# Second MoE of a talking-heads and double-MoE kernel: two token passes, seven block products in the second, weights narrowed once

## The chip, the cores and the metric

The kernel runs on one core of a Trainium2 chip. The metric is the device time of one execution in microseconds (us), lower being better. Engine names are those of the profile: PE is TensorE's matmuls, PEld its weight loads, DVE is VectorE, ACT ScalarE, POOL GpSimd and SP SyncE, which here only issues DMAs.

## The reference, cut to what matters

Three stages follow one another: an attention in which the heads are mixed before and after the softmax, a MoE with a SoLU and a layer norm (1792 tokens, 768 to 1024 to 768), and a second MoE with a squared ReLU (768 to 2048 to 768). The change is about the third, and prepares for it in the second.

```python
def _moe_ref(x, w_in, w_out, g_ln):
    h = x @ w_in
    e = np.exp(h - np.max(h, axis=-1, keepdims=True))
    solu = h * (e / (np.sum(e, axis=-1, keepdims=True) + 1e-09))
    mu = np.mean(solu, axis=-1, keepdims=True)
    var = np.mean((solu - mu) ** 2, axis=-1, keepdims=True)
    return ((solu - mu) / np.sqrt(var + 1e-06) * g_ln) @ w_out

def _moe2_ref(x, w_in, w_out):
    r = np.maximum(x @ w_in, 0.0)
    return (r * r) @ w_out
```

All weights of both MoEs come in as 64-bit floats; the kernel narrows them to 32 bits by moving bits about. Every product is made to 32-bit accuracy from two parts of each operand, a rounded one ("hi") and what is left ("lo"): hi*hi, hi*lo and lo*hi, so three matmuls where one would do.

## The kernel before, in words

Every engine does its instructions in the order in which the code issues them; nothing reorders them. `filler()` calls scattered through the code let pieces of background work (generators in `fill`) advance by one step.

**Attention** (up to about 405 us) reads q, k and v, and beside that narrows the first MoE's weights to DRAM, 48 pieces of 128x256 (`narrow_w1`). Each has an ACT square (L76), three DVE bit operations (L79, L83, L87) and two POOL operations (L96, L97).

**First MoE** (to 649 us) goes over 14 tiles of 128 tokens. For tile m, `h1` multiplies the tokens with w_in: 36 matmuls of 512 columns. `norm1` then takes the maximum (DVE L704), the exponential (ACT L707), the SoLU product (DVE L710), mean and variance (DVE L713, L715; POOL L717, L718), and normalises in place (DVE L720). `zt(m-1)` transposes the tile before on PE and splits it. From tile 4 on two `out1` calls follow, 24 matmuls of up to 384 columns each; a group of three tiles is one `out1` width. PE's order in a tile is thus h1(m), zt(m-1), out1, out1.

**Second MoE** (649 to 1120 us) walks over 8 slices e of 256 hidden units, and in each over five token groups (256 tokens, then four of 384; `GRP`). `h2(e, q)` makes the first product of a slice and a group, 18 matmuls for each of the two halves of the slice; ACT and DVE square it and split it into `g`; `y2(e, q)` makes the second product, 12 matmuls of 384 columns for each 128 tokens, and DVE adds it to a running sum `y` in SBUF (L955). The weights of slice e+1 are narrowed by `piece_w2` during slice e, 8 pieces of 128x384, with their hi and lo parts in the pool wi2 (left end of SBUF) for even slices and m2 (right end) for odd ones. The tokens, loaded once and split by `load_x2`, stay in SBUF: groups 0 and 1 in wi2, 2 to 4 in m2.

```python
    steps = [(e, q) for e in range(NE) for q in range(len(GRP))]
    h2(*steps[0])
    for i, (e, q) in enumerate(steps):
        ...
        if i + 1 < len(steps):
            h2(*steps[i + 1])
        y2(e, q)
```

PE thus always has the next group's first product between a group's squares and its second product.

Of the kernel before, what the change touches and what calls it, by code (L numbers as in the profile page):

```python
# [18 lines left out]
def kernel(  # L19
# [36 lines left out]
    const = ctx.enter_context(tc.tile_pool(name="const", bufs=1, side="left"))  # L56
    dram = ctx.enter_context(tc.tile_pool(name="dram", bufs=1, space=bass.MemoryType.DRAM))
# [601 lines left out]
    late.__exit__(None, None, None)  # L659

# [3 lines left out]
    m1_p = m1.__enter__()  # L664
    psi = tc.tile_pool(name="psi", bufs=1, side="left", space=PSUM, reuse_waits="tile")
# [34 lines left out]
    def norm1(m):  # L700
        ps = hps.pop(m)
        hv = ps.rearrange("p u f -> p (u f)")
        nm = m1_p.tile([128, 1], F32, tag="nm", name="nm", bufs=2)
        nc.vector.tensor_reduce(out=nm, in_=hv, op=ALU.max, axis=AX.X, negate=True)  # L704
        e = m1_p.tile([128, F1], F32, tag="e", name="e", bufs=2)
        sm = m1_p.tile([128, 1], F32, tag="sm", name="sm", bufs=2)
# [37 lines left out]
    def out1(grp, cc):  # L744
# [13 lines left out]
        o = m1_p.tile([128, GT * 128], F32, tag="o", name="o1", bufs=2)  # L758
        nc.scalar.copy(o[:, 0:width], ps[:, 0:width])
        nc.sync.dma_start(out=x2D[cc * 128:(cc + 1) * 128, t0:t0 + width], in_=o[:, 0:width])  # L760

    NTILE = NT // 128
    xr = {}
    wr = {}
    outs = []
    for m in range(NTILE):
# [5 lines left out]
        next(norm)  # L772
        if m > 0:
            zt(m - 1)
        run(norm)
# [17 lines left out]
    FE = 256
    NE = F2 // FE
    KE = FE // 128
    TG = 384
    GRP = [(0, NT % TG)] + [(t0, TG) for t0 in range(NT % TG, NT, TG)]
    x2 = {}
    w2 = {}

    def load_x2(g, pool):

        t0, n = GRP[g]
        t = pool.tile([128, 2, CC, n], F32R, name=f"x2_{g}")
        x2[g] = t
        rs = []
        for i in range(CC + 2):
            if i < CC:
                r = wi2_p.tile([128, TG], F32, tag="x2r", name="x2r", bufs=3)
                nc.sync.dma_start(out=r[:, 0:n], in_=x2D[i * 128:(i + 1) * 128, t0:t0 + n])  # L810
                rs.append(r)
            if i >= 2:
                c = i - 2
# [227 lines left out]
```

## Time and profile before

| what | value |
|---|---|
| median of 3 runs | 1122.43 us (1118.15 to 1130.88) |
| profiled execution, its own time | 1125.69 us |
| its span, first to last instruction | 1123.9 us |
| PE busy | 95% of the span |
| DVE, ACT, POOL busy | 61%, 42%, 37% |
| granted TensorE clock, mean | 0.983 |

The span is 1.8 us less than the execution's own time. Engine shares are means over three stages with different limits, so they are to be read by stage; matmuls are pipelined, and the pace of a run of them is read from the start of one run to the start of the next, divided by the count.

### The profile page before, as it was taken

Reading aid. Unit: us, or ns where it says so; the run is one execution under the profiler, and the core shown is the slowest. Engines: PE = TensorE matmul, PEld = TensorE weight load, DVE = VectorE, ACT = ScalarE, POOL = GpSimd, SP = SyncE. Lnnn points to the kernel's source line nnn. Section 1 sums busy time; section 2 is a strip of 40 time slices with the busy share of each in tenths; the row PEclk is TensorE's granted clock in tenths of the full one; section 3 lists DMA queues with packets and bytes.
Section 4 is the critical chain, followed back from the end, with each engine's and each line's share of the span. In section 5 each row is a group of like instructions: output and inputs, shape, how many; then the busy total and the mean of one; then the engine's idle time right before and its main releaser. Section 6 shows DMA issues by size and latency. Waiting matters only on the chain.

```text
span 1123.9 us, 30801 instructions
## 1 busy us (share of the span) xinstructions
PE 1067.6 (95%) x12920; PEld 926.9 (82%) x12920; DVE 680.8 (61%) x1201; ACT 468.9 (42%) x1026; POOL 418.7 (37%) x645
## 2 busy tenths in 40 slices
PE   8889889888898899999999999999999999999998
PEld 3566556655566688998989999999999999999998
DVE  2557676766676637443533786476676666766734
ACT  4556566666686634221211465322222223223210
POOL 2557797877584837111100653011111111111100
PEclk8989899999999999999999999999999999999999
DMA  6767688788676633111111653021111121111113
GB/s 179 206 187 236 210 232 246 240 233 237 182 226 180 189 103 116 57 31 55 36 36 48 193 183 113 29 57 43 57 57 57 50 63 43 57 57 57 29 71 127
DMA packets 95643, 135.00 MB, mean 120 GB/s; under 512 B 20720, under 2 KB 80368, under 8 KB 95504
## 3 DMA queue, kind: packets, MB, share of 16 engines
q1 hardware_dynamic: 86660, 108.50, 31.9%
q0 software_dynamic: 6464, 22.60, 7.1%
q10 hardware_dynamic: 2380, 1.93, 0.6%
q8 instruction: 102, 1.67, 0.6%
q14 instruction: 37, 0.30, 0.1%
HBM read 71.65 MB, written 22.81 MB: 84 GB/s over the span
## 4 chain that ended last, share of the span: by engine, by line
PE 85%; DMA 4%; issue 4%; ACT 3%; POOL 2%; DVE 1%; SPq 0%; ACTq 0%; POOLq 0%; DVEq 0%
PE ps_y L944 20%; PE ps_h L905 20%; PE ps_o L751 10%; PE ps_h L453 10%; PE ps_ring L293 6%; PE ps_ring L332 6%; PE ps_ring L202 5%; PE ps_pre L236 5%; DMA sdst<-ssrc 4%; ACT ssrc L209 1%; PE ps_tr L737 1%; ACT e L254 1%; POOL w1i L441 0%; PE ps_spare L481 0%; POOL sm L265 0%
## 5 line engine op out<-in xcount | busy, mean ns | idle before, releaser
L905 PE MATMUL ps_h<-x,ti 128*128 128x384 f32 (+1 forms) x1440 | 241.5, 325 | 0.0
L944 PE MATMUL ps_y<-to,g 128*128 128x384 f32 x1332 | 240.3, 337 | 0.2 <-ACT y L953 0.2
L905 PEld LDWEIGHTS ps_h<-x,ti 128*128 128x128 f32 x1440 | 236.5, 188 | 0.0
L944 PEld LDWEIGHTS ps_y<-to,g 128*128 128x128 f32 x1332 | 232.1, 188 | 2.2 <-DVE y L955 1.7
L293 PEld LDWEIGHTS ps_ring<-w,e 60*64 60x64 f32 (+1 forms) x5760 | 104.1, 139 | 70.3 <-issue 38.6
L312 DVE COPY at<-ps_ring 128x420 f32<-128x420 f32 x156 | 87.8, 610 | 102.6 <-PE ps_ring L293 102.5
L293 PE MATMUL ps_ring<-w,e 60*64 60x60 f32 (+2 forms) x5760 | 112.5, 223 | 30.0 <-issue 17.0
L209 ACT COPY ssrc<-ps_ring 128x896 f32<-128x896 f32 x92 | 82.5, 910 | 110.4 <-PE ps_ring L202 90.0
L913 ACT ACTIVATE r<-ps_h 128x384 f32<-128x384 f32 (+1 forms) x80 | 37.5, 469 | 215.2 <-PE ps_h L905 215.1
L453 PE MATMUL ps_h<-w1i,xs 128*128 128x512 f32 x504 | 120.5, 396 | 0.0
L751 PE MATMUL ps_o<-zt,w1o 128*128 128x384 f32 (+1 forms) x720 | 119.9, 325 | 0.0
L254 ACT ACTIVATE e<-ps_pre,nm 128x448 f32<-128x448 f32 x180 | 113.4, 641 | 13.8 <-DVE nm L247 12.1
L914 DVE SCALAR_TENSOR_TENSOR r<-ps_h,r 128x384 f32<-128x384 f32 (+1 forms) x80 | 42.4, 530 | 122.8 <-ACT r L913 122.7
L751 PEld LDWEIGHTS ps_o<-zt,w1o 128*128 128x128 f32 x720 | 116.8, 189 | 0.0
L453 PEld LDWEIGHTS ps_h<-w1i,xs 128*128 128x128 f32 x504 | 94.2, 188 | 21.5
L247 DVE TENSOR_REDUCE nm<-ps_pre 128x1 f32<-128x448 f32 x180 | 102.8, 611 | 15.1 <-PE ps_pre L236 15.0
L955 DVE TENSOR_TENSOR y<-ps_y,y 128x768 f32<-128x768 f32 x97 | 92.4, 953 | 31.8 <-PE ps_y L944 31.8
L861 POOL TENSOR_TENSOR ti<-wt,ti 128x384 fp32r<-128x384 f32 x32 | 34.4, 1075 | 206.6 <-ACT ti L860 206.6
L202 PE MATMUL ps_ring<-k,q 64*64 64x448 f32 x752 | 100.1, 569 | 8.0 <-issue 4.2
L332 PEld LDWEIGHTS ps_ring<-at,v 128*64 128x64 f32 x1536 | 77.7, 141 | 29.9 <-PE ps_pre L236 10.6
L236 PE MATMUL ps_pre<-sdst,wpre_bd 64*64 64x448 f32 x720 | 97.4, 580 | 5.1 <-issue 2.9
L332 PE MATMUL ps_ring<-at,v 128*64 128x120 f32 (+1 forms) x1536 | 85.2, 268 | 7.2 <-issue 4.3
(90 smaller groups left out, 1190.4 us busy)
## 6 DMA issues: line engine op xcount, KB each, us to landing
sdst<-ssrc SPq DMA_DIRECT2D x166, 210.0 KB
wr<-in_moe_w_in_dram SPq DMA_DIRECT2D x32, 384.0 KB
wr<-in_moe_w_out_dram SPq DMA_DIRECT2D x32, 384.0 KB
w1raw<-in_moe_w_in_dram POOLq DMA_DIRECT2D x24, 256.0 KB, 5.2
w1raw<-in_moe_w_out_dram POOLq DMA_DIRECT2D x24, 256.0 KB, 5.7
out_dram<-y SPq DMA_DIRECT2D x13, 384.0 KB
v<-in_v_dram POOLq DMA_DIRECT2D x12, 384.0 KB, 6.1
xraw<-xD SPq DMA_DIRECT2D x12, 384.0 KB
```

What stands on the lines that cost most here:

```text
L202: nc.tensor.matmul(out=ps[64 * u:64 * u + 64, e, 0:S], lhsT=qq[c][64 * e:64 * e + 64, p * n + u * half:p * n + u * half + 64], rhs=k[64 * ...
L209: (nc.vector.tensor_copy if dve else nc.scalar.copy)(ssrc[c][:, p:H:HP, :], ps[:, :, 0:S])
L236: nc.tensor.matmul(out=ps[b][64 * u:64 * u + 64, 0:S], lhsT=wpre_bd[64 * r:64 * r + m], rhs=ds[b][64 * r:64 * r + m], start=True, stop=True,)
L247: nc.vector.tensor_reduce(out=nm, in_=pres[s][b][:, 0:S], op=ALU.max, axis=AX.X, negate=True)
L254: nc.scalar.activation(out=e, in_=pres[s][b][:, 0:S], func=AF.Exp, bias=nms.pop((s, b)), scale=1.0, accum_out=sms[s][:, b:b + 1])
L293: nc.tensor.matmul(out=ps[64 * c:64 * c + 64, u, i0:i0 + ng * RH], lhsT=e[64 * u:64 * u + m, o:o + 64], rhs=w[64 * u:64 * u + m, b, g0:g0 ...
L332: nc.tensor.matmul(out=ps[64 * e:64 * e + 64, 0, q * 120:q * 120 + n], lhsT=t[:, g] if j < NJ else t[:, e, p], rhs=at[c][:, j * H + (g if ...
L453: nc.tensor.matmul(out=ps[:, u], lhsT=t[:, a, cc], rhs=w1i[cc][:, w, u * 512:(u + 1) * 512], start=(cc == 0 and a == 0 and w == 0), stop=( ...
L751: nc.tensor.matmul(out=ps[:, 0:width], lhsT=w1o[k][:, w, cc * 128:(cc + 1) * 128], rhs=zT[:, a, k, 0:width], start=(k == 0 and i == 0), st ...
L905: nc.tensor.matmul(out=ps[:, 0:n], lhsT=ti[:, w, cc, f * 128:(f + 1) * 128], rhs=x2[q][:, a, cc], start=(cc == 0 and i == 0), stop=(cc == ...
L944: nc.tensor.matmul(out=ps[:, u - us[0], 0:DM // 2], lhsT=g[:, a, f, o:o + 128], rhs=to[:, w, f, u * (DM // 2):(u + 1) * (DM // 2)], start= ...
L955: nc.vector.tensor_tensor(out=yo, in0=po, in1=yo, op=ALU.add)
```

## The change

The second MoE now makes two passes over 896 tokens each, and in each pass goes over all 8 slices (q = 0 to 15, `SEQ_P` and `SEQ`). A slice's first product is seen as a 2x2 block product: two halves of the hidden units (f), two halves of the tokens (t, 448 each), two halves of the 768 inputs (k). In the first pass (q < 8) each of the four result blocks is the sum of two block products ("22", "21", "12", "11"; 18 matmuls of 448 columns each). In the second pass the four blocks come from seven block products p1 to p7 of sums of blocks (9 matmuls each): POOL makes the sums of weights (`mix_w`), DVE the sums of tokens, once, to DRAM (`mix_second`), and DVE and ACT combine the products (`after`). p3, p2 and p4 are accumulated in PSUM on banks that already hold p5, p1 and p7.

The weights are no longer narrowed in the second MoE by `piece_w2`; `w2stream` narrows them once, to DRAM (w2iD, w2oD), 96 pieces of 128x256: 60 in the first MoE from its fifth tile on, six pieces (18 steps) a tile, and 36 in the first six slices of the first pass. A piece has an ACT square, one POOL operation and three DVE bit operations. Both passes read the narrowed weights back (`load_ra`, `load_ro`) and split them. The hi and lo parts for the second product (`to`) and the squares (`gt`) both lie in m2; the weights for the first product lie in wi2a at the left end, and the tokens in wi2 beside them, but for the blocks of p1, p5 and p6 in the second pass, which lie in m2. In the first MoE the normalisation moves from DVE to ACT, after a small DVE operation (`nb`). Tiles that were in `const` or m1 move to other pools.

```diff
-        nc.vector.tensor_scalar(
-            out=e, in0=e, scalar1=mv[:, 0:1], scalar2=rs, op0=ALU.subtract, op1=ALU.mult
+        nb = m1b_p.tile([128, 1], F32, tag="nb", name="nb", bufs=2)
+        nc.vector.scalar_tensor_tensor(
+            out=nb, in0=mv[:, 0:1], scalar=-1.0, in1=rs, op0=ALU.mult, op1=ALU.mult
         )
+        yield True
+        nc.scalar.activation(out=e, in_=e, func=AF.Identity, bias=nb, scale=rs)
...
+        def mask(i):
+            if i in todo:
+                t = ts[i] = home(i, False)
+                nc.scalar.activation(out=t, in_=words(i)[1].bitcast(F32), func=AF.Square)
+                nc.gpsimd.tensor_scalar(
+                    out=t, in0=t, scalar1=2.0**-30, scalar2=2.0 - 2.0**-23, op0=ALU.is_ge, op1=ALU.mult
+                )
...
+        for i in todo:
+            load(i + nr - 1)
+            mask(i + 2)
+            low, high = words(i)
+            bits = ts[i].bitcast(U32)
+            stt = nc.vector.scalar_tensor_tensor
+            stt(out=bits, in0=high, scalar=3, in1=bits, op0=ALU.logical_shift_left, op1=ALU.bitwise_and)
+            yield True
+            if ready:
+                store()
+            stt(out=bits, in0=high, scalar=0xC0000000, in1=bits, op0=ALU.bitwise_and, op1=ALU.bitwise_or)
+            yield True
+            stt(out=bits, in0=low, scalar=29, in1=bits, op0=ALU.logical_shift_right, op1=ALU.bitwise_or)
+            raws.pop(i)
+            ready.append(i)
+            yield True
...
+        steps2(rate(m, 4))
+        next(norm)
         if m > 0:
             zt(m - 1)
-        run(norm)
+        if m <= GT:
+            run(norm)
+        steps2(rate(m, 6))
...
+        pairs = PLAIN.get(name, ((name, name),))
+        for j, (tn, xn) in enumerate(pairs):
+            t = ti[q, tn]
+            for c in range(HC):
                 for i, (w, a) in enumerate(((0, 0), (0, 1), (1, 0))):
                     nc.tensor.matmul(
...
+                        out=bank[b][:, 0:HT],
+                        lhsT=t[:, w, c],
+                        rhs=xc[xn][:, a, c],
...
+    YO = [4, 5, 6, 3, 0, 1, 2]
+    SEQ = ["p1", "p6", 4, "p5", 5, "p7", 6, 3, 0, "p3", 1, 2, "p2", "p4"]
+    SEQ_P = ["22", 4, "21", 5, 6, 3, "12", 0, 1, 2, "11"]
...
+            at(3, split_ti, n, "p1")
+            at(3, mix_w, n, 0)
+            at(4, mix_w, n, 1)
+            at(5, split_ti, n, "p6")
+            at(6, split_ti, n, "p5")
+            at(7, lambda q: square(hs.pop(q), 1, 1), q)
+            at(7, split_ti, n, "p7")
+            at(8, split_to, q, 0)
+            at(10, split_ti, n, "p3")
+            at(11, split_to, q, 1)
+            at(11, load_ro, n)
+            at(12, split_ti, n, "p2")
+            at(13, split_ti, n, "p4")
+            at(13, load_ra, n + 1)
```

In `SEQ` and `SEQ_P` a number is a tile of 128 tokens whose second product (`y2`), that of the slice before, stands there; the work of `plan` is issued behind the place with its number.

On PE a slice of the second MoE stood so before (ps_h is the first product, ps_y the second, x the tokens, ti and to the weights of the first and second product):

```order
L905 MATMUL ps_h_12253<-x_0_9173,ti 128x256 x18
L905 MATMUL ps_h_12286<-x_0_9173,ti 128x256 x18
L944 MATMUL ps_y<-to,g 128x384 x36
L905 MATMUL ps_h_12360<-x_1_9354,ti 128x384 x18
L905 MATMUL ps_h_12391<-x_1_9354,ti 128x384 x18
L944 MATMUL ps_y<-to,g 128x384 x24
L905 MATMUL ps_h_12455<-x_2_9615,ti 128x384 x18
L905 MATMUL ps_h_12481<-x_2_9615,ti 128x384 x18
L944 MATMUL ps_y<-to,g 128x384 x36
```

A slice of the second pass now stands so, from p1 to p4 (xc is a block, or a sum of blocks, of the tokens):

```order
L1107 MATMUL ps_h_13407<-xc,ti 128x448 x9
L1107 MATMUL ps_h_13419<-xc,ti 128x448 x9
L1178 MATMUL ps_y<-to,gt 128x384 x12
L1107 MATMUL ps_h_13444<-xc,ti 128x448 x9
L1178 MATMUL ps_y<-to,gt 128x384 x12
L1107 MATMUL ps_h_13481<-xc,ti 128x448 x9
L1178 MATMUL ps_y<-to,gt 128x384 x36
L1107 MATMUL ps_h_13444<-xc,ti 128x448 x9
L1178 MATMUL ps_y<-to,gt 128x384 x24
L1107 MATMUL ps_h_13407<-xc,ti 128x448 x9
L1107 MATMUL ps_h_13481<-xc,ti 128x448 x9
```

Per slice and pass there are 63 matmuls of 448 columns here, 72 in the first pass, and over both passes 1080 for the 1440 of before; those of the second product are 1344 as before. The banks ps_h_13444, 13407 and 13481 come up twice, for the accumulated products.

On DVE a tile of the first MoE stood so before (nm to st is the normalisation up to mean and variance, zt the split of the tile before):

```order
L704 TENSOR_REDUCE nm<-ps_h 128x1
L708 TENSOR_SCALAR sm<-sm 128x1
L709 RECIPROCAL sm<-sm 128x1
L710 SCALAR_TENSOR_TENSOR e<-e,sm,ps_h 128x1024
L713 BN_STATS st<-e 128x6 x2
L715 BN_AGGR mv<-st 128x2
L740 TENSOR_TENSOR zt<-ps_tr,zt 128x4x128 x2
L720 TENSOR_SCALAR e<-e,mv,rs 128x1024
```

Now, from the statistics of a tile (from the fifth on) to the first steps behind the split (nraw is a raw piece of weights, nt its narrowed form):

```order
L725 BN_AGGR mv<-st 128x2
L828 SCALAR_TENSOR_TENSOR nt<-nraw,nt 128x256
L832 SCALAR_TENSOR_TENSOR nt<-nraw,nt 128x256
L834 SCALAR_TENSOR_TENSOR nt<-nraw,nt 128x256
L828 SCALAR_TENSOR_TENSOR nt<-nraw,nt 128x256
L731 SCALAR_TENSOR_TENSOR nb<-mv,rs 128x1
L753 TENSOR_TENSOR zt<-ps_tr,zt 128x4x128 x2
L832 SCALAR_TENSOR_TENSOR nt<-nraw,nt 128x256
L834 SCALAR_TENSOR_TENSOR nt<-nraw,nt 128x256
```

The normalisation has left DVE, and 18 narrowing steps a tile have come in, four of them ahead of `nb` and the split.

On SP's queue in the first pass, a slice's worth of DMAs now stands so; the second MoE's queue of before held the raw weights in the same way, but no reads of narrowed ones:

```order
L996 DMA ro<-w2oD 128x768 x2
L793 DMA nraw<-in_moe_w_in_dram 128x256
L985 DMA ra<-w2iD 128x3x256 x2
L811 DMA w2iD<-nt 128x256
L793 DMA nraw<-in_moe_w_in_dram 128x256
L811 DMA w2iD<-nt 128x256
L793 DMA nraw<-in_moe_w_out_dram 128x256
```

The reads ro and ra take up single buffers, and raw loads and stores of the stream stand behind them.

## Rows read from the trace of the kernel before

**Rows 1.** Stretches of the two MoEs: length, busy time by engine, PEclk, DMA share, GB/s.

```profile
core 0: us, PE busy (x) PEld busy (x) DVE busy (x) ACT busy (x) POOL busy (x), PEclk, DMA share, GB/s
446.90:604.70 157.80, 157.80 (x824) 142.57 (x822) 66.13 (x90) 34.04 (x62) 23.57 (x28) 1.00 0.14 43
...
648.70:1120.30 471.60, 471.42 (x2786) 469.12 (x2784) 300.52 (x493) 146.91 (x309) 72.92 (x69) 1.00 0.21 66
```

**Rows 2.** Second MoE, PE in order of time: start us, us, line, tiles, count.

```profile
701.97 4.39 PE L905 MATMUL ps_h<-x,ti 128*128 128x256 f32 x36
706.19 6.41 PE L944 MATMUL ps_y<-to,g 128*128 128x384 f32 x36
712.43 6.40 PE L905 MATMUL ps_h<-x,ti 128*128 128x384 f32 x36
...
781.55 6.52 PE L905 MATMUL ps_h<-x,ti 128*128 128x384 f32 x36
787.91 2.28 PE L944 MATMUL ps_y<-to,g 128*128 128x384 f32 x12
```

**Rows 3.** Matmuls by shape: count | busy us, mean ns | idle before.

```profile
L944 PE MATMUL ps_y<-to,g 128*128 128x384 f32 x1332 | 240.3, 337 | 0.2 <-ACT y L953 0.2
L905 PE MATMUL ps_h<-x,ti 128*128 128x384 f32 x1152 | 206.3, 336 | 0.0
...
L905 PE MATMUL ps_h<-x,ti 128*128 128x256 f32 x288 | 35.4, 281 | 0.0
```

**Rows 4.** First MoE, PE in order of time, one tile.

```profile
561.02 8.58 PE L453 MATMUL ps_h<-w1i,xs 128*128 128x512 f32 x36
569.44 1.03 PE L737 MATMUL ps_tr<-id_sb,e 128*128 128x128 f32 x8
570.23 8.57 PE L751 MATMUL ps_o<-zt,w1o 128*128 128x384 f32 x48
578.64 8.58 PE L453 MATMUL ps_h<-w1i,xs 128*128 128x512 f32 x36
```

**Rows 5.** First MoE, groups of instructions from 480 to 600 us.

```profile
L720 DVE TENSOR_SCALAR e<-e,mv,rs 128x1024 f32<-128x1024 f32 x7 | 13.9, 1983 | 0.0
...
L707 ACT ACTIVATE e<-ps_h,nm 128x1024 f32<-128x1024 f32 x7 | 7.8, 1117 | 64.1 <-DVE nm L704 64.1
```

**Rows 6.** Start of the first MoE, PE's transposes of tile 0 and their wait.

```profile
418.10 1.06 PE L737 MATMUL ps_tr<-id_sb,e 128*128 128x128 f32 x8 [1.15 <-DVE e L720]
```

**Rows 7.** Narrowing of 128x256 pieces in the attention: groups of instructions.

```profile
L96 POOL TENSOR_SCALAR w1sq<-w1sq 128x256 f32<-128x256 f32 x48 | 41.0, 854 | 4.0
...
L83 DVE SCALAR_TENSOR_TENSOR w1t<-w1raw,w1t 128x256 uint32<-128x256 uint32 x48 | 21.4, 445 | 1.4
...
L76 ACT ACTIVATE w1sq<-w1raw 128x256 f32<-128x256 f32 x48 | 19.8, 448 | 0.0
```

**Rows 8.** The same DVE operation: duration ns min/median/max, first and last start.

```profile
L83 DVE SCALAR_TENSOR_TENSOR w1t<-w1raw,w1t x48: 408/426/940, 65.9 to 324.6; 128x256 uint32<-128x256 uint32 x48
```

**Rows 9.** A stretch of the attention.

```profile
100.00:200.00 100.00, 89.44 (x2271) 59.62 (x2267) 72.30 (x162) 63.04 (x150) 79.55 (x144) 0.95 0.78 230
```

**Rows 10.** Second MoE, groups of instructions on DVE, POOL and ACT.

```profile
L955 DVE TENSOR_TENSOR y<-ps_y,y 128x768 f32<-128x768 f32 x97 | 92.4, 953 | 31.8 <-PE ps_y L944 31.8
...
L914 DVE SCALAR_TENSOR_TENSOR r<-ps_h,r 128x384 f32<-128x384 f32 x64 | 35.6, 557 | 104.3 <-ACT r L913 104.3
...
L861 POOL TENSOR_TENSOR ti<-wt,ti 128x384 fp32r<-128x384 f32 x32 | 34.4, 1075 | 206.6 <-ACT ti L860 206.6
...
L919 ACT CAST g<-r 128x384 fp32r<-128x384 f32 x64 | 32.8, 512 | 29.1 <-DVE r L914 29.1
```

**Rows 11.** SP's own waits: in total us, times, longest us.

```profile
SPq L832 <- DVE wt L87: 187.7, 25, 21.6
```

**Rows 12.** The last instructions: PE, the last sum on DVE.

```profile
1118.06 2.25 PE L944 MATMUL ps_ye<-to,g 128*128 128x384 f32 x12
...
1120.35 0.56 DVE L955 TENSOR_TENSOR y<-ps_ye,y 128x384 f32<-128x384 f32 x1 [0.49 <-PE ps_ye L944]
```

More of the change, by code (lines that the diff above doesn't have):

```diff
@@ L664 @@
     m1_p = m1.__enter__()
+    m1b = tc.tile_pool(name="m1b", bufs=1, side="right", reuse_waits="tile")
+    m1b_p = m1b.__enter__()
     psi = tc.tile_pool(name="psi", bufs=1, side="left", space=PSUM, reuse_waits="tile")
@@ L763, with home1, rate, steps2 @@
+    def home1(i, raw):
+        if raw:
+            return m1b_p.tile([128, WP], I64, tag="nraw", name="nraw", bufs=5)
+        return m1b_p.tile([128, WP], F32, tag="nt", name="nt", bufs=5)
+    stream = w2stream(range(FIRST), 5, home1)
+    NTILE = NT // 128
+    def rate(m, n):
+        return 0 if m <= GT else n if m < NTILE - 1 else n // 2
+    def steps2(n):
+        for _ in range(n):
+            next(stream, None)
     xr = {}
@@ L783 @@
             outs += [((m - 1) // GT - 1, cc) for cc in range(CC)]
-        for _ in range(2):
+        for i in range(2):
             if outs:
                 out1(*outs.pop(0))
+            if i == 0:
+                run(norm)
+            steps2(rate(m, 4))
+    outs += [((NTILE - 1) // GT, cc) for cc in range(CC)]
     wi1b.__exit__(None, None, None)
     wi1.__exit__(None, None, None)
+    wi2a = tc.tile_pool(name="wi2a", bufs=1, side="left", reuse_waits="tile")
+    wi2a_p = wi2a.__enter__()
@@ L791 @@
+    prep2 = prepare()
+    next(prep2)
+    steps2(4)
+    out1(*outs.pop(0))
+    zt(NTILE - 1)
+    run(stream)
+    m1b.__exit__(None, None, None)
     wi2 = tc.tile_pool(name="wi2", bufs=1, side="left", reuse_waits="tile")
     wi2_p = wi2.__enter__()
[L793 to L813, printed above, removed]
-                nc.scalar.copy(t[:, 0, c], rs[c][:, 0:n])
-                eng = nc.vector if g > 1 and c % 2 else nc.gpsimd
-                eng.tensor_tensor(
-                    out=t[:, 1, c], in0=rs[c][:, 0:n], in1=t[:, 0, c].bitcast(F32), op=ALU.subtract
-                )
-            yield True
@@ L863 @@
[L863 to L870 removed]
     for i, (g, cc) in enumerate(outs):
+        if i:
+            next(prep2, None)
         out1(g, cc)
[L873 to L878 removed]
@@ L879 @@
-    while fill:
-        filler()
-    for _ in x2q:
-        pass
-    for _ in x2q1:
-        pass
+    run(prep2)
     ps1.__exit__(None, None, None)
@@ L904, in h2, with prod @@
+    bank = {}
+    us = {}
+    hs = {}
+    low = []
+    def prod(q, name):
+        b = BANK[name]
+        first = name not in ("p3", "p2", "p4")
+        if first:
+            bank[b] = ps2_p.tile([128, 512], F32, tag=f"b{b}", name="ps_h2", bufs=1)
+        pairs = PLAIN.get(name, ((name, name),))
+        for j, (tn, xn) in enumerate(pairs):
+            t = ti[q, tn]
+            for c in range(HC):
                 for i, (w, a) in enumerate(((0, 0), (0, 1), (1, 0))):
                     nc.tensor.matmul(
-                        out=ps[:, 0:n],
@@ new lines, in prod, with lows @@
+                        lhsT=t[:, w, c],
+                        rhs=xc[xn][:, a, c],
+                        start=(first and j == 0 and c == 0 and i == 0),
+                        stop=(j == len(pairs) - 1 and c == HC - 1 and i == 2),
+                        skip_group_check=not first,
+                    )
+    def lows():
+        while low:
+            r, f, t = low.pop(0)
+            hi, lo = [gt[:, a, f, t * HT:(t + 1) * HT] for a in range(2)]
+            nc.vector.tensor_tensor(out=lo, in0=r, in1=hi.bitcast(F32), op=ALU.subtract)
@@ L985 @@
+    assert not parts
+    for x in YO:
+        y2(NQ - 1, x)
+        lows()
+    assert next(mx, None) is None
     ps2.__exit__(None, None, None)
```

507 lines of the change are left out of this document (359 added, 148 removed).

## The prediction, made before the changed kernel ran

> **What bounds the kernel now.** I read the stretches first, since the change touches the second MoE and the tail of the first [rows 1]. From 648.7 to 1120.3 us PE is busy 471.42 of 471.60 us, at PEclk 1.00, which is the 2.4 GHz level; from 446.9 to 604.7 it is busy all of 157.80 us. DVE has 300.52 of 471.60 us there and 66.13 of 157.80 here, POOL 72.92 and 23.57. So PE's stream of matmuls sets the time in both stages, and a change is worth what it takes off that stream, as long as no other engine comes to stand in its way. DVE, at 64% in the second MoE and 42% in the first, is the one to watch.
>
> Next is the pace of matmuls, from start to start of runs [rows 2]. 36 of 256 columns take 706.19 - 701.97 = 4.22 us, 117.2 ns each; 36 of 384 take 712.43 - 706.19 = 6.24 us, 173.3 ns. In every other slice, for three of its four wide groups, 36 of 384 take 787.91 - 781.55 = 6.36 us, 176.7 ns: the same shape at a slow pace, and it goes with the pool in which the slice's weights lie. 36 of 512 in the first MoE take 569.44 - 561.02 = 8.42 us, 233.9 ns [rows 4]. From 256 to 384 columns a column costs 56.1 / 128 = 0.438 ns, so there is a fixed part of only some 5 ns: what counts is columns, and fewer, wider matmuls save little.
>
> **First product of the second MoE: what goes.** The counts are 288 of 256 columns and 1152 of 384 [rows 3]: 288 x 0.1172 = 33.8 us, and 1152 x (5/8 of 0.1733 + 3/8 of 0.1767) = 201.1 us, together 234.9. Now there are 8 x 72 = 576 matmuls in the first pass and 8 x 63 = 504 in the second, all of 448 columns. No row has that shape. From the fast 384 and 0.438 ns a column, one is 173.3 + 28.1 = 201.4 ns; at least it is 173.3 + 64 / 2.4 = 200.0; at most, half way between the slow 384 and the first MoE's 512, 205.3. I take 201.4, since it is nearest to the row of the same stage. 1080 x 0.2014 = 217.5 us, so **17.4 us go** (13.2 to 18.9). The first pass gives about a tenth of it: 576 x 0.2014 = 116.0 against half of before, 117.5. The rest is the eighth block product, which the second pass leaves out.
>
> The Trainium skill (TensorE: Matmul & The Clock Gate, "Back-to-back issue gap") gives a gap of N / 2.4 + 2.5 ns: 109.2, 162.5 and 189.2 ns for 256, 384 and 448 columns. The rows are 7% above it at 256 and 384, so the rows decide; by the page the saving would be 218.6 - 204.3 = 14.3 us, an estimate.
>
> **Second product.** Its 1344 matmuls stay. What the stage has beside the first product is 471.6 - 234.9 = 236.7 us, or 176.1 ns each with all waits, against 173.3 in slices whose two operands lie in m2. Now weights and squares always lie there: 0 to 3.8 us, taken as 2.5.
>
> **First MoE.** A tile takes 578.64 - 561.02 = 17.62 us of PE [rows 4]. DVE has 66.13 / 157.80 of that, 7.4 us; the normalisation leaves it (1.98 us [rows 5]) and 18 narrowing steps come in. The same operation on the same 128x256 piece took 0.445 us in the attention [rows 7]: 8.0 us. Together 13.4, with some 1.3 us of waiting for the exponential (ACT 1.12 us [rows 5]) 14.7 of 17.62. ACT gets about 1.1 for the normalisation and 6 x 0.448 for squares beside its 34.04 / 157.80 x 17.62 = 3.8: 7.6. POOL gets 6 x 0.854 beside 2.6: 7.7. All stay under PE's 17.62, and PE has a whole tile of room for what they make: the normalised tile m is wanted by the transposes that stand behind h1(m+1). So nothing is charged here. If that cover goes, each 1 us over 17.62 costs about 10 us, for ten tiles. SP carries in a tile 6 x 384 KB of narrowing and about 0.8 MB of before, 3.1 MB in 17.62 us or some 180 GB/s; the attention moved 230 GB/s in a stretch with the same kind of pieces [rows 9]. The transposes of tile 0 waited 1.15 us for the DVE normalisation [rows 6]; on ACT it should end earlier: 0 to 1.2 us gained, taken as 0.5.
>
> **What waits could come in the second MoE.** A slice is 72 x 0.2014 + 84 x 0.1735 = 29.1 us of PE in the first pass and 27.3 in the second. From [rows 10], DVE in the first pass: 7 sums of 0.953, 4 splits of about 0.65 and 18 steps of 0.445, 17.3 us; ACT 12 operations of about 0.6 on squares, and 9 us of splits and masks; POOL 4 x 1.075, two wide splits of about 2, and 6 x 0.854, 13.4. In the second pass POOL has 11 operations of 1.075 and the two wide ones, 15.8; DVE 7 sums, 6 additions (0.557 at 384 columns) and 4 splits, 13.2. None is near PE's time. By latency: p1 of the next slice needs the bank of p2, whose first reader is ACT; p4 stands between them, 9 x 0.2014 = 1.8 us, against about 0.6 for the read. The squares for tile 3 (p4's the last) are wanted 13 us after p4.
>
> What is left is SP's queue. ro and ra have single buffers, so their DMAs wait for POOL's splits at a slice's end (SP waited so before, up to 21.6 us at a time [rows 11], while PE lost next to nothing), and the raw loads behind them are some 4 us later. ACT's mask then waits for its load, DVE's steps for the mask, and behind those steps stands the sum that frees one of two PSUM buffers of the second product, which has 2.1 us a tile. I bound this by 0 and 2.5 us for each of six slices, and the two places where tokens are loaded or mixed (ahead of the stage, and in slices 6 and 7) by 0 and 2 us each: 0 to 19, taken as 3, as pieces are loaded three ahead and a mask is made two pieces, 6 us and more, before it is used. The end is as before: last matmuls at 1118.06, sum, store [rows 12].
>
> **The sum.** -17.4 - 2.5 - 0.5 + 3 = -17.4 us. The profiled execution took 1125.69 us, so 1108.3; the median of the runs is 3.3 us under it, 1122.4, and there I forecast **1105 us**. 1% of it is 11.2 us, about what a measurement of this kernel can tell from no change: faster means under 1111.2, slower over 1133.6.
>
> **Rivals.**
> First, *the wide matmuls run at the slow pace*, because the tokens of three block products and the weights lie at opposite ends of SBUF as in the slow rows: 205.3 ns, 221.7 us, and the second product gains nothing. -13.2 - 0.5 + 3 gives 1112 us. For it: even slices and all of h1 show such a pace. Against: in the first pass both operands lie at the left. Chance 0.17.
> Second, *SP's queue makes PE wait* in most slices, as above, about 2 us in six slices and 3 at the hand-overs, so 15 in place of 3: 1117 us. Against: DVE has 40% to spare to catch up. Chance 0.12.
> Third, the slower side: *DVE comes to bound the first MoE.* Its steps read two SBUF tensors while POOL makes masks and splits. In the attention, with POOL busy 79.55 of 100 us [rows 9], the step was 0.445 on average over a least time of 0.408, once 0.940 [rows 8]. A tile is over 17.62 us from (17.62 - 6.7) / 18 = 0.607 us a step on. If DVE waited out all of POOL's 7.7 us, a tile would be 22.4 us: 4.8 x 10 = 48 us more, 1153 us. The step's mean lies far from 0.607, so 0.07. The Trainium skill (SBUF — State Buffer, "Who interferes with whom") says that a VectorE instruction with two SBUF inputs and a GpSimd one that reads SBUF block each other for the whole instruction; the maximum of 0.940 agrees, the mean says it is rare.
> Fourth, *the matmuls don't go*: excluded, as the built order has 1080 of them.
>
> **How the numbers follow.** The forecast, 1098 to 1111, has 0.60; the slow pace 0.17, half of it under 1111; the queue 0.12; DVE 0.07; a time under 1098 (all bounds at their good end and the first MoE better) 0.04. The range 1096 to 1120 leaves out the third rival, part of the second's upper end and the lowest times, together below 0.2. Faster: 0.60 + 0.04 + 0.06 = 0.70; slower: 0.07; within 1%: 0.23.
>
> **What would show it.** The 448-column matmuls 201 ns apart, 3.6 us for 18 of them; second MoE some 455 us long; 17.6 us a tile in the first MoE with DVE near 80% of it; PE's idle time in the second MoE under 5 us. I am wrong if a tile of the first MoE is longer than 18 us, if ps_y waits for DVE's sum at the slices' starts in the first pass, or if p1 waits for ACT.

## The result and the profile after

The changed kernel takes 1129.47 us (median of 20 runs, 1123.03 to 1140.18) beside 1123.08 us for the kernel before (20 runs, 1117.87 to 1130.88): a ratio of **1.0058** [1.0032, 1.0084], where 1105 us were forecast. Run again beside other kernels it gave 1.0021 [0.9989, 1.0054]. So it is no faster: it is 0.2 to 0.6% slower, the smaller of the two inside its interval. Its profiled execution took 1126.69 us, with a span of 1124.9 us at a clock of 0.982.

The stretches of the changed kernel that answer to [rows 1] (columns as there):

```profile
core 0: us, PE busy (x) PEld busy (x) DVE busy (x) ACT busy (x) POOL busy (x), PEclk, DMA share, GB/s
452.00:610.00 158.00, 157.75 (x825) 142.64 (x824) 129.66 (x249) 65.04 (x128) 94.98 (x84) 1.00 0.60 179
655.10:1121.30 466.20, 456.39 (x2426) 438.52 (x2424) 252.57 (x343) 204.62 (x388) 224.07 (x184) 0.99 0.35 115
```

The second MoE is 466.2 us long in place of 471.6, not 455, and PE is idle for 9.8 us of it, where it lost 0.2 before. The first MoE keeps PE busy as it did, with DVE at 82%, DMA at 0.60.

Its matmuls by shape, against [rows 3] (count | busy us, mean ns | idle before):

```profile
L1178 PE MATMUL ps_y<-to,gt 128*128 128x384 f32 x1332 | 244.6, 338 | 9.2 <-DVE y L1189 5.3 <-ACT y L1187 3.6 <-POOL to L1044 0.3
L1107 PE MATMUL ps_h<-xc,ti 128*128 128x448 f32 x1080 | 227.3, 365 | 0.6 <-ACT h L1123 0.6
```

Nearly all of PE's waits stand before the second product (9.2 of 9.8 us), and two thirds of them are two waits. They are seen in order of time (start us, us, line, tiles, count, idle before):

```profile
567.41 8.55 PE L459 MATMUL ps_h<-w1i,xs 128*128 128x512 f32 x36
...
585.02 5.29 PE L459 MATMUL ps_h<-w1i,xs 128*128 128x512 f32 x22
...
687.56 3.89 PE L1178 MATMUL ps_y<-to,gt 128*128 128x384 f32 x12 [3.61 <-ACT y L1187]
691.29 3.81 PE L1107 MATMUL ps_h<-xc,ti 128*128 128x448 f32 x18
...
720.45 3.81 PE L1107 MATMUL ps_h<-xc,ti 128*128 128x448 f32 x18
724.10 6.41 PE L1178 MATMUL ps_y<-to,gt 128*128 128x384 f32 x36
730.34 7.46 PE L1107 MATMUL ps_h<-xc,ti 128*128 128x448 f32 x36
737.63 2.24 PE L1178 MATMUL ps_y<-to,gt 128*128 128x384 f32 x12
...
838.28 3.64 PE L1178 MATMUL ps_y<-to,gt 128*128 128x384 f32 x12 [3.11 <-DVE y L1189]
841.75 0.57 PE L1107 MATMUL ps_h<-xc,ti 128*128 128x448 f32 x2
...
867.86 2.38 PE L1178 MATMUL ps_y<-to,gt 128*128 128x384 f32 x12 [0.95 <-DVE y L1189]
871.09 2.34 PE L1178 MATMUL ps_y<-to,gt 128*128 128x384 f32 x12 [0.85 <-DVE y L1189]
```

From start to start, 448 columns take 3.65 / 18 = 202.8 ns and 7.29 / 36 = 202.5 ns, 384 columns 6.24 / 36 = 173.3 ns: both products have the pace that was forecast. A tile of the first MoE takes 585.02 - 567.41 = 17.61 us, as before. The two long waits cost more than their length. The 12 matmuls that follow the first take 691.29 - 687.56 = 3.73 us in place of 2.08, those behind the second 3.47, since the granted clock had fallen to the lower of its two levels, 1.2 GHz, for most of them (PEclk, a mean over the stretch, is the column ahead of the DMA share):

```profile
687.50:691.30 3.80, 3.74 (x13) 3.74 (x14) 1.25 (x3) 1.88 (x5) 3.34 (x4) 0.55 0.45 111
...
838.20:841.70 3.50, 3.42 (x12) 3.46 (x13) 1.95 (x3) 0.04 (x1) 0.00 (x0) 0.58 0.77 254
...
720.40:730.30 9.90, 9.90 (x56) 9.63 (x55) 7.45 (x11) 5.42 (x11) 6.43 (x6) 1.00 0.26 83
```

With that, 3.61 + 1.65 + 3.11 + 1.39 = 9.8 us go in two places. Adding up what each start-to-start gap in the second MoE has over a matmul's own time, every gap over 0.26 us counted, gives some 14 us: 5.4 in slice 1, 4.7 in slice 6, 2.3 in slice 7 and 2 in smaller gaps.

**Slice 1 (683.8 us).** ACT in order of time:

```profile
678.68 0.43 ACT L803 ACTIVATE nt<-nraw 128x256 f32<-128x256 f32 x1 [4.15 <-DMA nraw<-in_moe_w_in_dram]
679.02 0.79 ACT L1187 COPY y<-ps_y 128x768 f32<-128x768 f32 x1
685.37 0.43 ACT L803 ACTIVATE nt<-nraw 128x256 f32<-128x256 f32 x1 [5.56 <-DMA nraw<-in_moe_w_in_dram]
686.39 0.43 ACT L803 ACTIVATE nt<-nraw 128x256 f32<-128x256 f32 x1 [0.59 <-DMA nraw<-in_moe_w_in_dram]
686.73 1.48 ACT L1187 COPY y<-ps_y 128x768 f32<-128x768 f32 x2
```

and SP, which issues that load:

```profile
671.75 3.72 SPq L996 DMA_DIRECT2D ro<-w2oD  x2
675.51 0.42 SPq L793 DMA_DIRECT2D nraw<-in_moe_w_in_dram  x1
677.89 1.53 SPq L985 DMA_DIRECT2D ra<-w2iD  x2
679.51 0.43 SPq L793 DMA_DIRECT2D nraw<-in_moe_w_in_dram  x1
```

In a pass's first slice the sums of y are copies, and they are on ACT (L1187). ACT stood at a mask whose load SP could not issue before 679.51, because ro and ra stood ahead of it and waited for POOL's splits. So two finished PSUM buffers were not read, and PE had no third. The load of 679.51, with both transfers of ra issued just ahead of it, was also slow: ACT had its data 5.9 us after the issue, where that of 675.51 was there after 3.2 us.

**Slices 6 and 7.** DVE in order of time:

```profile
829.35 0.95 DVE L1189 TENSOR_TENSOR y<-ps_y,y 128x768 f32<-128x768 f32 x1
833.83 0.63 DVE L925 TENSOR_TENSOR xb<-xb 128x448 f32<-128x448 f32 x1 [3.53 <-DMA xb<-x2D]
835.32 1.95 DVE L925 TENSOR_TENSOR xb<-xb 128x448 f32<-128x448 f32 x3 [0.86 <-DMA xb<-x2D]
837.18 1.82 DVE L1189 TENSOR_TENSOR y<-ps_y,y 128x768 f32<-128x768 f32 x2
...
866.06 0.88 DVE L978 TENSOR_TENSOR xc<-xr,xc 128x448 fp32r<-128x448 f32 x1 [8.16 <-ACT xc L977]
866.87 0.94 DVE L1189 TENSOR_TENSOR y<-ps_y,y 128x768 f32<-128x768 f32 x1
```

and SP:

```profile
824.98 1.52 SPq L985 DMA_DIRECT2D ra<-w2iD  x2
826.55 3.23 SPq L811 DMA_DIRECT2D w2oD<-nt  x5
829.83 3.77 SPq L917 DMA_DIRECT2D xb<-x2D  x8
```

The mixes of the second pass's tokens (L925) wait for their load, which SP issued from 829.83 us on, behind ra and five stores; the sums of y stand behind them. In slice 7 the splits (L977 on ACT, which waits 7.4 us for xr, and L978 on DVE) do the same.

So the second MoE is 5.4 us shorter and not 17, and the first is 1.4 us longer from tile 0's transposes on, which leaves a kernel that should still be some 4 us faster. What made it slower lies in the attention, whose code is the same, and only the runs showed it.

### The profile page after: what moved, and what is told of

It is laid out like the page before. It is cut to its first block, busy times and chain, and to the rows that moved or that the text cites. A ratio compares the mean times of both kernels' runs of the same rounds, so it can differ in the third digit from the quotient of the medians.

```text
span 1124.9 us, 30957 instructions
## 1 busy us (share of the span) xinstructions
PE 1055.5 (94%) x12560; PEld 898.9 (80%) x12560; DVE 680.0 (60%) x1213; ACT 561.0 (50%) x1171; POOL 629.8 (56%) x808
## 4 chain that ended last, share of the span: by engine, by line
PE 74%; DMA 8%; issue 7%; POOL 4%; ACT 3%; DVE 2%; SPq 1%; ACTq 0%; POOLq 0%; DVEq 0%
PE ps_y L1178 18%; PE ps_h L1107 14%; PE ps_o L764 9%; PE ps_h L459 9%; PE ps_ring L338 7%; PE ps_ring L299 7%; PE ps_pre L242 5%; PE ps_ring L208 4%; DMA sdst<-ssrc 4%; DMA ra<-w2iD 1%; ACT ssrc L215 1%; POOL ti L1036 1%; PE ps_tr L750 1%; POOL nt L804 1%; DMA v<-in_v_dram 1%
## 5 line engine op out<-in xcount | busy, mean ns | idle before, releaser
L1178 PE MATMUL ps_y<-to,gt 128*128 128x384 f32 x1332 | 244.6, 338 | 9.2 <-DVE y L1189 5.3
L1178 PEld LDWEIGHTS ps_y<-to,gt 128*128 128x128 f32 x1332 | 235.5, 190 | 12.5 <-ACT y L1187 3.9
L1107 PE MATMUL ps_h<-xc,ti 128*128 128x448 f32 x1080 | 227.3, 365 | 0.6 <-ACT h L1123 0.6
L1107 PEld LDWEIGHTS ps_h<-xc,ti 128*128 128x128 f32 x1080 | 201.9, 188 | 15.0 <-ACT h L1123 1.0
L804 POOL TENSOR_SCALAR nt<-nt 128x256 f32<-128x256 f32 x96 | 111.5, 1161 | 64.3 <-ACT nt L803 55.2
L299 PE MATMUL ps_ring<-w,e 60*64 60x60 f32 (+2 forms) x5760 | 110.2, 221 | 26.7 <-issue 17.5
L338 PEld LDWEIGHTS ps_ring<-at,v 128*64 128x64 f32 x1536 | 80.7, 145 | 36.9 <-issue 12.9
L1036 POOL TENSOR_TENSOR ti<-ra,ti 128x384 fp32r<-128x384 f32 x56 | 59.5, 1075 | 89.9 <-ACT ti L1035 88.3
L1120 DVE TENSOR_TENSOR gt<-h,gt 128x448 fp32r<-128x448 f32 x64 | 48.9, 764 | 96.3 <-ACT gt L1125 91.6
L338 PE MATMUL ps_ring<-at,v 128*64 128x120 f32 (+1 forms) x1536 | 88.8, 274 | 14.3 <-issue 7.5
```

What stands on the lines that cost most here:

```text
L299: nc.tensor.matmul(out=ps[64 * c:64 * c + 64, u, i0:i0 + ng * RH], lhsT=e[64 * u:64 * u + m, o:o + 64], rhs=w[64 * u:64 * u + m, b, g0:g0 ...
L338: nc.tensor.matmul(out=ps[64 * e:64 * e + 64, 0, q * 120:q * 120 + n], lhsT=t[:, g] if j < NJ else t[:, e, p], rhs=at[c][:, j * H + (g if ...
L804: nc.gpsimd.tensor_scalar(out=t, in0=t, scalar1=2.0**-30, scalar2=2.0 - 2.0**-23, op0=ALU.is_ge, op1=ALU.mult)
L1107: nc.tensor.matmul(out=bank[b][:, 0:HT], lhsT=t[:, w, c], rhs=xc[xn][:, a, c], start=(first and j == 0 and c == 0 and i == 0), stop=(j == ...
L1178: nc.tensor.matmul(out=ps[:, u - u2[0], 0:DM // 2], lhsT=gt[:, a, f, o:o + 128], rhs=w[:, v, f, u * (DM // 2):(u + 1) * (DM // 2)], start= ...
```

## The experiments

The theories as the runs went on: **W**, the block product left out pays its full time in the second MoE, and waits of PE take it back; **P**, it doesn't pay; **Q**, the wait of slice 1 is SP standing at ro and ra; **D**, DVE or POOL simply have too much work there; **A** (later **A2**), where the constants and the DRAM tensors lie slows the attention; **S**, the attention only scatters; **L**, the tiles of the attention lie 32 bytes off, and that slows its shuffles; **C**, the constants' own place does it. A ratio is to the kernel before, timed beside it. Ratios of one and the same program differ by 0.3 to 0.5%: the kernel before against itself gives 0.9974 (e9), and e1 and e10 are one program, with 1.0008 and 1.0053. The ratios of e1 to e4, which share their eleven runs of the kernel before, may thus all lie some 0.4% low.

**e1: the places alone.** The kernel before with the constants in the new pool and four DRAM tensors declared.

```diff
+    mixc = tc.tile_pool(name="mixc", bufs=1, side="right")
+    mixc_p = mixc.__enter__()
-    mask_sb = const.tile([128, 2, RH], F32, name="mask_sb")
+    mask_sb = mixc_p.tile([128, 2, RH], F32, name="mask_sb")
... 
+    w2iD = dram.tile([DM, F2], F32, name="w2iD")
```

> The kernel before, with only the changed kernel's placement ahead of the second MoE: the small tiles of the attention in a pool at the right end of SBUF, and the four further DRAM tensors, never used. Theory W (the gain was spent on PE's waits in the second MoE, 14 us in the profile of the changed kernel, and the 6 us later start of the first MoE there is the attention's own scatter): the same as before, within 3 us. Theory A (the changed kernel's attention is slower by some 6 us because its tiles lie elsewhere): 6 us slower than before, about 1129, and the first MoE starts near 412 us.

1.0008 [0.9981, 1.0035]. I took that as an end of theory A, too soon: it was six runs, beside eleven of the kernel before that came out high (1130.3 us, where it took 1127.0 beside e5 to e8 and beside e9 to e12).

**e2: no narrowing in the second MoE.** It leaves out the last 36 pieces and reads slices 0 to 2's weights in their place.

```diff
-            f0 = (q % NE) * FE
+            f0 = (q % NE) % 5 * FE
...
-                r0 = (q % NE) * FE + f * 128
+                r0 = (q % NE) % 5 * FE + f * 128
...
-    stream = w2stream(range(FIRST, len(w2pieces)), 4, home2)
+    stream = iter(())
```

> The changed kernel without the 36 pieces that are narrowed in the first pass; slices 5 to 7 read the narrowed weights of slices 0 to 2, so a part of the weights isn't used. Theory W: the wait in slice 1 (5.3 us with the slow clock behind it) goes and that of slice 6 gets shorter, 6 to 10 us less than the changed kernel, 1120 to 1124. Theory A or theory P (the block products do not pay, as the second pass has other limits): within 3 us of the changed kernel, 1127 to 1132.

0.9892 [0.9849, 0.9936]; second MoE 456.4 us, the wait of slice 1 gone, 1.7 us left of slice 6's 3.3. By the trace that is 9.8 us less than the changed kernel, inside what theory W expected; the ratio, of few runs, says 14 to 19 us, more than W and the trace account for.

**e3: ra and ro on POOL's queue.**

```diff
-                nc.sync.dma_start(
+                (nc.gpsimd if q > 1 else nc.sync).dma_start(
                     out=t,
                     in_=w2iD[...]
-                nc.sync.dma_start(out=t, in_=w2oD[r0:r0 + 128, :])
+                (nc.gpsimd if q else nc.sync).dma_start(out=t, in_=w2oD[r0:r0 + 128, :])
```

> The changed kernel with the reads of narrowed weights (ra from the third slice on, ro from the second) issued on POOL's queue, so that raw loads and stores on SP's queue no longer stand behind POOL's splits. Theory Q (PE waits in slice 1 because SP's queue stands still): the wait in slice 1 goes, 4 to 6 us less than the changed kernel, 1123 to 1126; those in slices 6 and 7 stay. Rival D (the raw loads are late because ra and ro fill the DMA engines ahead of them): slice 1 still waits 3 us or more, and the time stays within 2 us of the changed kernel.

0.9933 [0.9898, 0.9968]; second MoE 461.4 us, no wait in slice 1, that of slice 6 still there (4.6 us from start to start). Q holds for slice 1: all narrowing is still done. The edit takes away both halves of the wait, the late issue and the transfer behind ra, and does not part them.

**e4: the eighth product back.** Nine matmuls more in each slice of the second pass, their result unread.

```diff
+                if x == "p5":
+                    eighth(q)
```

> The changed kernel with an eighth block product of nine matmuls in each slice of the second pass, whose result nothing reads. Theory W: PE bounds the second pass, so all of it is paid, 72 x 0.2015 = 14.5 us more than the changed kernel, about 1144. Theory P (something else bounds the second pass): less than 5 us more.

1.0129 [1.0099, 1.016]. The second MoE is 483.3 us, 17.1 us more than the changed kernel's 466.2, and its gaps add up to 2.7 us more. So the product left out pays 17.1 - 2.7 = 14.4 us by the traces, against 72 x 0.202 = 14.5. The ratio is 0.7 to 1.1% above those of the changed kernel, 8 to 12 us. Either way theory P falls.

**e5: the changed kernel again**, unedited.

> The changed kernel, nothing edited, beside the other three and on the same chip. Theory W (the block product left out pays its 17 us in the second MoE, and waits of TensorE there take most of it back) expects the same places as in its first profile: one wait of 3 to 4 us in slice 1 behind ACT's copy of y, one of 3 to 5 us in slice 6 and two of about 1 us in slice 7 behind DVE's sums, a second MoE of 462 to 468 us, and 0.998 to 1.008 of the time of the kernel before. Theory T (the waits of the first profile were of one execution) expects them in other slices, or with other sizes.

1.0021 [0.9989, 1.0054]; the same waits in the same slices, 3.5 us for ACT and 5.8 for DVE, second MoE 468.1 us. They belong to the program, not to one execution.

**e6: mixes later, tokens earlier.**

```diff
         parts = [load_xb(1, 0), load_xb(1, 1)]
-        yield True
+        load_xc(1, "p1")
+        for _ in range(3):
+            yield True
...
-                if i % 2:
+                if i == 1:
                     yield True
...
+        load_xc(1, "p6")
+        yield True
...
-            load_xc(*parts[0][0])
-            load_xc(*parts[HC][0])
```

> The changed kernel with the mixes of the second pass's tokens given to DVE two slots later in slice 6, and the first tokens of the second pass asked for in slice 6 instead of in slice 7. All the work is done. If the waits of slices 6 and 7 are DVE and ACT standing in order behind a transfer (theory W), the wait of 3.1 us in slice 6 and the two of about 0.9 us in slice 7 go, with about 1.4 us of a lower clock behind the first; the wait of slice 1 stays; the second MoE takes 459 to 461 us and the kernel 0.994 of the changed one. If TensorE waits there for something else, for instance because DVE has too much work in these slices (theory D), the waits move two slots later and the time stays within 0.2% of the changed kernel's.

0.9969 [0.994, 0.9997], so 0.9948 of the changed kernel's ratio; second MoE 459.3 us, and the waits of slices 6 and 7 are gone without work taken away. D falls for them, by the trace; the two ratios' intervals overlap.

**e7: e3 and e6 together.**

> The late mixes and the early tokens of the run before this one, together with the weight loads of the second MoE on the DMA queue of POOL. All the work is done. Theory W expects nearly all of the 14 us back: no wait over 1.5 us anywhere in the second MoE, 453 to 456 us for it, and 0.986 to 0.991 of the kernel before. Theory D expects waits of more than 5 us in sum to come up elsewhere, and 0.993 or more.

0.9938 [0.9905, 0.9971]. PE's waits are gone (2.7 us in sum, second MoE 455.9 us), yet the time is 0.994 and not 0.988. Here the account by trace and the measured time parted: 15.7 us less in the second MoE and 1.4 us more in the first should give 14, and 7 came.

**e8: copies of y on DVE.**

```diff
-                nc.scalar.copy(yo, po)
+                nc.vector.tensor_copy(yo, po)
```

> The changed kernel with the copies of y of each pass's first slice on DVE in place of ACT. All the work is done. If TensorE waits in slice 1 because ACT's copy stands behind a mask that waits for a late weight load (theory W, as its trace reads), the wait of 3.6 us goes, or shrinks to under 1.5 us, since DVE's own steps stand behind masks two pieces older, and the kernel takes 0.995 of the changed one. If DVE's steps are held up as long by the same masks (rival), the wait stays at 2 us or more and is for DVE's copy, and the time is that of the changed kernel within 0.2%.

0.9987 [0.9955, 1.0019], 0.9966 of the changed kernel's ratio, which is not clear of it; by the trace the wait of slice 1 is gone and the second MoE takes 461.2 us. DVE there:

```profile
684.03 0.96 DVE L1187 COPY y<-ps_y 128x768 f32<-128x768 f32 x1 [0.85 <-PE ps_y L1178]
...
688.86 0.42 DVE L828 SCALAR_TENSOR_TENSOR nt<-nraw,nt 128x256 uint32<-128x256 uint32 x1 [1.80 <-POOL nt L804]
```

The copy waits for PE now, not PE for the copy, while the late mask still holds up DVE's own steps by 1.80 us.

**e9 to e12: theory A once more, in its parts.** The kernel before unedited (e9), e1 again (e10), the pool alone (e11), the DRAM tensors alone (e12).

> The kernel before, nothing edited, as a second profile of it and as a measure of the scatter. In the changed kernel and its variants the traces account for some 3 to 15 us less in the second MoE and 1.4 us more in the first, and the times came out 5 to 7 us above that sum in one comparison and on it in another. Theory A2 (where the small constants and the DRAM tensors lie costs the attention 4 to 6 us on average) expects this run's attention to end at 417 to 420 us and a ratio of 0.998 to 1.002. Theory S (the attention's end scatters by some 8 us from execution to execution, in every kernel alike) expects any end between 417 and 426 us and the same ratio.

> The kernel before with the constants in their new pool and the four DRAM tensors declared and not used; all the work is done, in the old order. Theory A2 expects 1.003 to 1.006 and an attention that ends at 421 to 426 us; theory S expects 0.997 to 1.003.

> The kernel before with the constants in their new pool alone, no new DRAM tensors; all the work is done. If theory A2 holds by the place of the constants in SBUF: 1.003 to 1.006; if it holds by the place of the DRAM tensors, and under theory S: 0.997 to 1.003.

> The kernel before with the four DRAM tensors declared and not used, the constants where they were; all the work is done. If theory A2 holds by the place of the DRAM tensors: 1.003 to 1.006; if by the place of the constants, and under theory S: 0.997 to 1.003.

0.9974 [0.9949, 0.9999], 1.0053 [1.0023, 1.0082], 1.0045 [1.0016, 1.0074] and 0.9981 [0.9953, 1.001]. So the pool costs 5 to 6 us beside the runs of the kernel before, and 7 to 9 us (0.64 to 0.79%) beside e9 and e12, with no instruction changed, and the DRAM tensors cost nothing. The end of the attention (the start of tile 0's transposes) is no measure of it in one profile: it fell at 414.9 to 430.0 us in these four, and at 424.1 in e12, whose median was among the low ones.

**e13 to e16: the pool's size.** The pool holds 736 bytes a partition, 2.875 x 256. By the program's addresses ssrc, sdst and k, on the right side, start at multiples of 256 bytes in the kernel before; the pool puts them 32 bytes past one. A pad of 32 bytes mends that in e11 (e13), in the changed kernel (e14) and in e7 (e15); e16 puts 32 bytes under the right side of the kernel before, so that they start 32 bytes short of one, and moves no constant.

```diff
     g_sb = mixc_p.tile([128, F1 // 128], F32, name="g_sb")
+    mixc_p.tile([128, 8], F32, name="pad_sb")
```

> The kernel before with the constants in their new pool, and 32 unused bytes a partition beside them, so that the tiles of the attention lie on multiples of 64 bytes again; all the work is done. If the shift of the tiles by 32 bytes slows the shuffles (theory L), the 1792-byte packets take 91 to 93 ns each again and the time is 0.997 to 1.002 of the kernel before. If it is the constants' own place (theory C), the packets stay at 97 ns or the time at 1.004 to 1.007.

> The changed kernel with the same 32 unused bytes; all the work is done. Theory L expects 0.995 to 0.999 of the kernel before, 4 to 6 us under the changed kernel as it is, with the waits of slices 1, 6 and 7 where they were; theory C expects the changed kernel's 1.002 to 1.006.

> The changed kernel with its waits removed (late mixes, early tokens, weight loads on the queue of POOL) and the 32 unused bytes; all the work is done. Theories W and L together expect what the traces sum to: 15 us less in the second MoE, 1.4 us more in the first and nothing in the attention, 0.986 to 0.990 of the kernel before. Theory C expects 0.992 to 0.995 as without the pad.

> The kernel before with a pool of 32 unused bytes a partition on the right side and the constants where they were; all the work is done. Only the tiles of the right side move, by 32 bytes. Theory L expects the shuffles' packets at 96 to 98 ns and 1.003 to 1.007; theory C expects 91 to 93 ns and 0.997 to 1.002.

| kernel | ssrc, sdst and k from a multiple of 256 | ratio | 1792-byte packets of the attention, mean (median) ns |
|---|---|---|---|
| before (e9) | 0 | 0.9974 [0.9949, 0.9999] | 91.6 (74) |
| e12, DRAM tensors | 0 | 0.9981 [0.9953, 1.001] | 91.6 (74) |
| e13, pool and pad | 0 | 1.001 [0.9977, 1.0042] | 91.6 (74) |
| e14, changed and pad | 0 | 0.999 [0.9956, 1.0023] | 92.7 (74) |
| e15, waits removed and pad | 0 | **0.9876** [0.9834, 0.9918] | 94.3 (74) |
| e11, pool | 32 past | 1.0045 [1.0016, 1.0074] | 97.9 (78) |
| e10, pool and tensors | 32 past | 1.0053 [1.0023, 1.0082] | 97.4 (80) |
| e1, the same program as e10 | 32 past | 1.0008 [0.9981, 1.0035] | 97.0 (78) |
| changed kernel (e5) | 32 past | 1.0021 [0.9989, 1.0054] | 96.5 (79) |
| e16, before and shift | 32 short | 1.0081 [1.0047, 1.0116] | 97.1 (78) |

The last column is worked out from the packet records of the first 400 us of each trace, some 22,000 packets of 1792 bytes: 21,504 of the shuffles sdst<-ssrc and 768 of SP's six loads of k. The median is 74 ns in all six traces with the old offset and 78 to 80 in all twelve with the new one, e1's too, whose ratio does not show it. Theory L's ratios are met but for e16, which came out above its 1.003 to 1.007; in e14 the waits of the second MoE are where they were (9.2 us for ACT's copy and DVE's sums, in slices 1, 6 and 7). At the start, where the shuffles stand on the path, the queue's share of the DMA engines shows it (packets, MB, share of 16 engines, 0 to 28 us), for the kernel before,

```profile
q1 hardware_dynamic: 2517, 3.41, 42.6%
```

for the pool with its pad (e13),

```profile
q1 hardware_dynamic: 2506, 3.39, 42.6%
```

and for the shift alone (e16):

```profile
q1 hardware_dynamic: 2506, 3.39, 49.0%
```

The same packets and bytes hold the engines 15% longer. (Over all traces it is 42.6 to 45.5% with the old offset, e14 and e15 highest, and 46.5 to 49.0 with the new one.) The shift of 32 bytes is the cause of the longer packets and of the longer time, by e16 and e13 (1.0081 and 1.001, 8 us apart); the constants' own place costs nothing that these runs can tell.

That the time is lost in the attention shows over all 18 traces: it ends at 418.6 us on average in the six with the old offset and at 423.7 in the twelve with the new one, while in the kernels with the old code the first MoE (230.4 to 230.6 us) and the second (469.6 to 472.1) are no longer at the new offset. That it is lost through the packets is argued, not shown. ACT's copies into ssrc take 905 ns (median) in e13 and e16 alike, so no slower access by ACT is seen; but the granted clock over an execution is lower too, 0.983 to 0.985 on average in the runs of e10, e11 and e16 against 0.988 in those of e9, e12 and e13, and no run parts the two.

**e15** is the fastest version: 1110.04 us, a ratio of 0.9876. Its second MoE and the waits of PE in it:

```profile
core 0: us, PE busy (x) PEld busy (x) DVE busy (x) ACT busy (x) POOL busy (x), PEclk, DMA share, GB/s
...
656.10:1110.70 454.60, 452.87 (x2426) 435.81 (x2424) 250.23 (x343) 205.00 (x388) 261.43 (x242) 1.00 0.36 117
```

```profile
PE ps_y L1183 <- DVE y L1194: 0.8, 2, 0.4
PE ps_h L1112 <- ACT h L1128: 0.6, 1, 0.6
PE ps_y L1183 <- POOL to L1049: 0.3, 1, 0.3
```

454.6 us is what the prediction gave for this stage, and the kernel's gain is 1.2% of the 1.6% forecast: some 14 us, where 17.0 us less in the second MoE and 1.4 us more in the first give 15.6, inside the interval.

## Why the prediction was wrong, step by step

**First and second product: right.** 1080 x some 0.202 = 218.2 us against 217.5, second product at 173.3 ns. e4 shows the block product's 14.4 us by itself, e15 the whole stage. The gap of the Trainium skill (TensorE: Matmul & The Clock Gate, "Back-to-back issue gap"), 189.2 ns for 448 columns, was 7% under this row as well.

**The waits, "0 to 19, taken as 3": the step that failed.** They measured some 14 us, and the rival that priced them at 15, SP's queue, was put at 0.12. It was right in the sum and not in the places: it had 2 us in most slices, by way of DVE's steps and the sum behind them. The reason given for the small value was that a mask is made two pieces before it is used. That is true of DVE's steps, and beside the point: ACT issues in order, so the wait of a mask that nobody needs yet holds up whatever stands behind it, and in a pass's first slice that is the read of PSUM (e8 and e3 show it from two sides). Slices 6 and 7 were priced together at 0 to 2 us; with a load issued at 829.83 and its user standing first in DVE's order, slice 6 alone cost 4.7 us and slice 7 another 2.3 (e6). The lower clock after the two long waits, nearly a third of their price, had no term at all.

**A term was missing: the attention, put at nothing without a reason.** The line "Tiles that were in const or m1 move to other pools" was read as free. By e10 to e13 and e16 the move costs 5 to 9 us, by an offset of 32 bytes. With it, and 0.8 us for the first MoE below, -17.4 + 11 + 0.8 + 7 is about +1 (-1 to +3), and the changed kernel measured +2.4 to +6.4 us; the rest is no more than what comparisons of one program differ by, 3 to 5 us.

**First MoE: nearly right.** A tile takes 17.61 us, so nothing is lost in the steady part, and the third rival falls. From tile 0's transposes to the second MoE it takes 232.0 us against 230.6, by waits for POOL's splits in the first tiles (0.60 and 0.25 us are seen). The 1.15 us of [rows 6] ahead of the transposes are gone. Together about +0.3 in place of -0.5. The cover was thinner than worked out (groups of 480 to 600 us):

```profile
L804 POOL TENSOR_SCALAR nt<-nt 128x256 f32<-128x256 f32 x40 | 47.7, 1192 | 7.2 <-ACT nt L803 4.6
...
L832 DVE SCALAR_TENSOR_TENSOR nt<-nraw,nt 128x256 uint32<-128x256 uint32 x41 | 27.5, 672 | 1.2
L834 DVE SCALAR_TENSOR_TENSOR nt<-nraw,nt 128x256 uint32<-128x256 uint32 x40 | 19.2, 481 | 1.4
L828 DVE SCALAR_TENSOR_TENSOR nt<-nraw,nt 128x256 uint32<-128x256 uint32 x41 | 17.6, 429 | 0.0
```

POOL's mask took 1.19 us and not 0.854, DVE's steps (27.5 + 19.2 + 17.6) / 122 = 0.527 us and not 0.445; the limit was 0.607. The rule of the Trainium skill that DVE with two SBUF inputs and POOL hold each other up (SBUF — State Buffer, "Who interferes with whom") is borne out here by the two of them together, L832 above all: of its 41 steps in this stretch the five beside no POOL instruction took 0.43 us at most, the others up to 1.96.

**The rest of "what would show it".** PE's idle time was to stay under 5 us and was 9.8; "ps_y waits for DVE's sum in the first pass" was named as a sign of being wrong, and came in slices 6 and 7; p1 waited for ACT, the third sign, once, for 0.63 us at the start of the second pass.

What stays open is which of the right side's tiles matters, ssrc or sdst or the loads of q and k, since all moved together; whether a multiple of 64 or 128 bytes would do, since ssrc, sdst and k lay on multiples of 256 in every kernel with the short packets; and how much of the 5 to 9 us is the packets and how much the lower clock beside them.

## What to carry to other kernels

Where an engine works in order, a background step is not free because its result is wanted late: ask what stands behind it while it waits for its load, and who reads PSUM there. Before calling a move of tiles free, work out the offsets that it gives to everything allocated after it; here a pool of 736 bytes cost a third to a half of the change's gain, and 32 bytes of padding gave it back. When a trace's account and the measured ratio part, run the parts that change no instruction too, and with enough runs.

## What the runs showed of the hardware

DMA packets of 1792 bytes between SBUF tiles that start 32 bytes past a multiple of 256 (32 short of one in e16) took 78 to 80 ns (median), against 74 between tiles on multiples of 256, and 96 to 98 against 92 to 94 on average. After a wait of PE of 3.1 to 3.6 us the granted clock was 0.55 to 0.58 for the next 3.5 to 3.8 us, while after waits of 0.95 and 0.85 us the next 12 matmuls took 871.09 - 867.86 - 0.85 = 2.38 us and 873.27 - 871.09 = 2.18 us, near the 2.08 of full speed. POOL's mask of a 128x256 piece took 1.19 us beside a DVE at 82%, 0.854 in the attention [rows 7].
